# Column norms with a quarter of the array per chunk: 32 columns of ones as weights, 512 moving squares, partial sums added at the end

## The chip, the core and the metric

The kernel runs on one core of a Trainium2 chip. The metric is the device time of one execution in microseconds (us). Five engines work beside each other, each with its own in-order queue: TensorE (PE in the profile; its weight loads are listed apart as PEld), VectorE (DVE), ScalarE (ACT), GpSimd (POOL) and SyncE (SP). Sixteen DMA engines move data between the main memory and the on-chip buffer SBUF. Matmuls write to a second on-chip memory, PSUM, which is read by VectorE and ScalarE.

## The reference

There are four batches. In each, q, k and v have 6400 rows and 256 columns. The columns of q and k are divided by their norms over the 6400 rows, a 256x256 matrix of cosines is formed and turned into weights by a softmax, and v is multiplied by it. A mixture of eight adapters with two experts per row follows.

```python
qn = q / (np.linalg.norm(q, axis=1, keepdims=True) + 1e-06)
kn = k / (np.linalg.norm(k, axis=1, keepdims=True) + 1e-06)
s = kn.transpose(0, 2, 1) @ qn / tau
...                                   # softmax over the last axis: a
x = (v @ a).reshape(B * S, D)
logits = x @ w_gate                   # top 2 of 8, weights w by softmax
out = x + sum over the two experts of w * ((x @ A[e]) @ B[e])
```

The norms are the part of this that the change is about: for each of 256 columns of q and 256 of k, the sum of 6400 squares, in each batch.

## The kernel before

**Tiling.** The 6400 rows of a batch are 50 chunks of 128 rows; the rows lie on the 128 partitions. q and k come in tiles of 10 chunks (`qk`, four buffers), v in tiles of up to 18 chunks (`vt`, three buffers). GpSimd issues these loads, which convert from fp32 to bf16 on the way. Outputs are collected in groups of up to ten chunks (`ys`, nine buffers) and stored by ScalarE's queue, the last ones by SyncE's.

**First part of a batch.** Squares are made for two chunks at a time (`square`, L199), by ScalarE or, in batch 0, in turn by VectorE and ScalarE, into a pool of four tiles `sq` of 128 x (q and k) x 2 chunks x 256. `gram` (L211) adds k-transposed times q of one chunk to the PSUM tile `acc` with two matmuls of 256 moving columns (L217). `norm` (L222) adds the sums of squares of one chunk to the PSUM tile `nrm`. It has two forms. In batch 0 the weights are 128x128 ones and the 512 squares of the chunk (256 of q, 256 of k) move (L228): every partition of `nrm` then holds all 512 sums. In batches 1 to 3 the squares are the weights, four blocks of 128 columns, and one column of ones moves (L234): four matmuls, and the 512 sums lie in four columns of `nrm`, one column of the matrix per partition.

**The chain.** When a batch has all its chunks, seven functions `chain0` to `chain6` turn `acc` and `nrm` into the attention weights and the adapters' weights. `chain0` (L241) takes the logarithm of the sums on ScalarE (L252) and half its exponential (L254), that is the root. In batch 0 VectorE first takes the diagonal of `nrm` (L247) and sums it (L250), to bring the sums to one per partition. `chain1` makes the reciprocals and scales `acc`, `chain2` spreads the norms of q over the partitions with an fp32 matmul of ones (L276), `chain3` takes the exponential, `chain4` to `chain6` transpose and multiply.

**Second part of a batch.** Pairs of chunks of v are transposed on TensorE (L366), copied out of PSUM by VectorE (L377) or ScalarE (L375), multiplied for the gates (L387), for the adapters' z (L472) and for y (L488); z is gated on VectorE (L476), transposed back (L496), and added to y (L508), which ScalarE copies to `ys` (L512).

**Order.** The order of the work is written out by hand: batch 0's first part runs alone, then a loop over "slots" deals out, in each slot, one pair of chunks of the second part of a batch and two or three chunks of the first part of the next. The first parts of batches 1, 2 and 3 lie in the slots 0 to 20, 24 to 45 and 49 to 67 of 100; the functions of the chain follow in the slots behind each. In a slot the squares are put in first, then `chain0` to `chain3`, then the z matmuls, half the slot's `gram` and `norm` work (`gram_part`, L547), the y matmuls and transposes, and the other half. Since each engine's queue is in order, an instruction that waits holds up all that stands behind it there. Stores are held back by seven groups (`DEFER`, L52 and L601) up to the end of batch 3's first part and then let go by and by.

Of the kernel before, what the change touches and what calls it, by code (L numbers as in the profile page):

```python
# [8 lines left out]
FP32 = mybir.dt.float32  # L9
BF16 = mybir.dt.bfloat16  # L10
AX = mybir.AxisListType
OP = mybir.AluOpType
# [4 lines left out]
def kernel(  # L17
# [16 lines left out]
    nc = tc.nc  # L34
    B, N, C = q.shape
    P = 128
    NC = N // P
    CC = C // P
# [23 lines left out]
    const = ctx.enter_context(tc.tile_pool(name="const", bufs=1))  # L62
    qk_pool = ctx.enter_context(tc.tile_pool(name="qkp", bufs=QKB))
    v_pool = ctx.enter_context(tc.tile_pool(name="vp", bufs=VB))
    sq_pool = ctx.enter_context(tc.tile_pool(name="sqp", bufs=4))
# [18 lines left out]
    for b, (first, last) in GRAM.items():  # L84
        n = last - first + 1
# [43 lines left out]
    def load_more(limit=1000):  # L129

        while limit and at_load[0] < len(loads):
            _, kind, b, s, o, parts = loads[at_load[0]]
            if (kind, b, s) not in where:
                n = len(left[kind])
                if n >= bufs[kind] and left[kind][n - bufs[kind]]:
                    return
                where[kind, b, s] = n
                left[kind].append(PC if kind == "qk" else VP[s])
                if kind == "qk":
                    t = qk_pool.tile([P, 2, PC, C], BF16, tag="qk", name="qk")  # L140
                else:
                    t = v_pool.tile([P, max(VP), C], BF16, tag="v", name="vt")
                tiles[kind][b, s] = t
            t = tiles[kind][b, s]
            c0 = s * PC if kind == "qk" else sum(VP[:s])
            for m in parts:
                if kind == "qk":
                    nc.gpsimd.dma_start(t[:, 0, o:o + m, :], q_v[b, :, c0 + o:c0 + o + m, :])  # L148
                    nc.gpsimd.dma_start(t[:, 1, o:o + m, :], k_v[b, :, c0 + o:c0 + o + m, :])
                else:  # L150
                    nc.gpsimd.dma_start(t[:, o:o + m, :], v_v[b, :, c0 + o:c0 + o + m, :])  # L151
                o += m
            at_load[0] += 1
            limit -= 1
# [14 lines left out]
    ones_bf = const.tile([P, P], BF16)  # L169
    nc.vector.memset(ones_bf, 1.0)  # L170
    ones_f = const.tile([P, P], FP32)
    nc.vector.memset(ones_f, 1.0)
    neg_inv_tau = const.tile([P, 1], FP32)
    nc.vector.memset(neg_inv_tau, -inv_tau)
    for c in range(0, FIRST, 2):
# [6 lines left out]
    ident_f = const.tile([P, P], FP32)  # L182
# [14 lines left out]
    acc, nrm, sqs = {}, {}, {}  # L197

    def square(b, c, eng):  # L199

        s, o = divmod(c, PC)
        t = tiles["qk"][b, s]
        sq = sq_pool.tile([P, 2, 2, C], BF16, tag="sq", name="sq")
        sqs[b, c] = sq
        src = t[:, :, o:o + 2, :]
        if eng == "act":
            nc.scalar.activation(sq, src, ACT.Square)  # L207
        else:
            nc.vector.tensor_tensor(out=sq, in0=src, in1=src, op=OP.mult)  # L209

    def gram(b, c):  # L211
        if c == 0:
            acc[b] = ps_acc.tile([P, CC, C], FP32, tag="acc", name="acc")
        s, o = divmod(c, PC)
        t = tiles["qk"][b, s]
        for ic in range(CC):
            nc.tensor.matmul(  # L217
                acc[b][:, ic, :], t[:, 1, o, ic * P:(ic + 1) * P], t[:, 0, o, :],
                start=(c == 0 and ic == 0), stop=(c == NC - 1), skip_group_check=True)
        used("qk", b, c, 1)  # L220

    def norm(b, c):  # L222
        if c == 0:
            nrm[b] = ps_nrm.tile([P, 512], FP32, tag="nrm", name="nrm")
        sq = sqs[b, c - c % 2]
        if b == 0:

            nc.tensor.matmul(nrm[b].rearrange("p (w d) -> p w d", w=2), ones_bf, sq[:, :, c % 2, :],  # L228
                             start=(c == 0), stop=(c == NC - 1))
            return  # L230
        for w in range(2):
            for ic in range(CC):
                j = w * CC + ic
                nc.tensor.matmul(  # L234
                    nrm[b][:, j:j + 1], sq[:, w, c % 2, ic * P:(ic + 1) * P], ones_bf[:, 0:1],
                    start=(c == 0 and j == 0), stop=(c == NC - 1), skip_group_check=True)


    st = {}

    def chain0(b):  # L241
        d = st.setdefault(b, {})
        sums = nrm[b][:, 0:4]
        if b == 0:
            dq = sq_pool.tile([P, 4 * C], BF16, tag="sq", name="dq").bitcast(FP32).rearrange(
                "p (j d) -> p j d", j=4)
            nc.vector.tensor_tensor(out=dq, in0=nrm[b].rearrange("p (j d) -> p j d", j=4),  # L247
                                    in1=ident_f[:, None, :].to_broadcast([P, 4, P]), op=OP.mult)
            sums = const.tile([P, 4], FP32, name="sums")
            nc.vector.tensor_reduce(out=sums, in_=dq, axis=AX.X, op=OP.add)  # L250
        lnn = bat.tile([P, 4], FP32, name="lnn")
        nc.scalar.activation(lnn, sums, ACT.Ln)  # L252
        rt = bat.tile([P, 4], FP32, name="rt")
        nc.scalar.activation(rt, lnn, ACT.Exp, scale=0.5)  # L254
        d["rt"] = rt
# [71 lines left out]
    def chain6(b):  # L327
        d = st[b]
        a_bf = bat.tile([P, CC, C], BF16, name="a_bf")
        for ic in range(CC):  # L330
# [3 lines left out]


    CHAIN = [(chain0, 0.0), (chain1, 0.9), (chain2, 0.75), (chain3, 0.0), (chain4, 0.55),
             (chain5, 0.65), (chain6, 0.5)]


    groups = []  # L340
    for b in range(B):
        f = 0
        for n in [5, 5, 5, 5, 3, 2] if b == B - 1 else [GRP] * (NPAIR // GRP):
            g = {"b": b, "f": b * NPAIR + f, "n": n, "ready": False}
# [187 lines left out]
    for c in range(0, NC, 2):  # L532
        square(0, c, "act" if (c // 2) % 2 else "dve")
        gram(0, c)
        gram(0, c + 1)
        load_more()
        if c >= 4:
            norm(0, c - 4)
            norm(0, c - 3)
    for c in range(NC - 4, NC):  # L540
        norm(0, c)
    for f, _ in CHAIN:
        f(0)
        if f is chain3:
# [2 lines left out]
    def gram_part(items):  # L547
        for b, c in items:
            gram(b, c)
            if c >= 2:  # L550
                norm(b, c - 2)
            if c == NC - 1:
                norm(b, c - 1)
                norm(b, c)

    micro = []
    at_chain = {}
# [14 lines left out]
    zq, dq = None, None  # L572
    while nz < NPT or zq is not None or dq is not None:
# [10 lines left out]
        if f in (chain0, chain1, chain2, chain3):  # L584
            f(fb)
# [5 lines left out]
        if zq is not None:  # L591
            gz_t(zq, "act" if slot >= NPT else "dve")
        gram_part(items[:h])
        if dq is not None:
            y_mm(dq)
# [4 lines left out]
        dq, zq = zq, u  # L600
# [4 lines left out]
        if 0 < slot <= NPT and slot - 1 == groups[slot - 1]["f"] + groups[slot - 1]["n"] - 1:  # L605
# [3 lines left out]
            ops[0][1]()  # L609
            micro += ops[1:]  # L610
        gram_part(items[h:])
        if f in (chain4, chain5, chain6):
            f(fb)
# [42 lines left out]
```

## Time and profile before

| what | value |
|---|---|
| median of 3 runs | 255.92 us (255.84 to 256.08) |
| the profiled execution | 255.87 us |
| its span, first to last instruction | 254.1 us |
| busy: TensorE, VectorE, ScalarE, GpSimd | 220.4, 152.7, 176.1, 33.0 us |
| norm matmuls, batches 1 to 3 (L234) | 600, 35.9 us listed as busy |
| norm matmuls, batch 0 (L228) | 50, 15.8 us listed as busy |
| main memory read and written | 78.91 and 26.21 MB |

The span is what the profile covers; the time has some 1.8 us around it. In the profile the row of digits cuts the span into 40 slices, and each digit is the busy share in tenths. The chain of work goes back from the last instruction to what released each step. A busy time is the sum of listed durations, with overlaps inside a group counted once; the duration of a matmul includes the time until its result is out, so matmuls that follow one another overlap, and what one costs the queue is the distance between the starts.

### The profile page before, as it was taken

The numbers are of one execution on the slowest core, as the hardware profiler recorded it, in microseconds if no ns is written. First come the engines' busy times: TensorE is split into PE (matmuls) and PEld (weight loads), VectorE is DVE, ScalarE is ACT, GpSimd is POOL, SyncE is SP. The second block draws the span as 40 slices with busy tenths as digits, with TensorE's granted clock in tenths as the row PEclk, the third lists the DMA queues.
The fourth block names the chain that finished last, engine by engine and source line by source line (L and its number), as shares of the span: only waits on it lengthen the run. The fifth ranks groups of instructions, "written<-read, shape, count | busy, mean of one in ns | idle before, by whom it ended". The sixth has DMA issues, their size and how long they took to land.

```text
span 254.1 us, 7393 instructions
## 1 busy us (share of the span) xinstructions
PE 220.4 (87%) x3106; PEld 190.2 (75%) x3106; DVE 152.7 (60%) x577; ACT 176.1 (69%) x290; POOL 33.0 (13%) x67
## 2 busy tenths in 40 slices
PE   0787793985999999999999989999999899999950
PEld 0444461775899978989999778989997799998940
DVE  1322235453567678685776876767587876778720
ACT  3434344776488698887878778888867777887860
POOL 8131221112112100110110202000000200000000
PEclk9999998696899999999999999999999999999997
DMA  7999999999999999999999999999999999999995
GB/s 213 223 217 215 212 216 214 213 216 216 210 214 215 223 207 215 218 212 214 215 220 211 214 270 259 236 296 281 255 291 292 389 326 362 414 420 426 423 412 220
DMA packets 13745, 66.80 MB, mean 263 GB/s; under 512 B 2576, under 2 KB 2704, under 8 KB 10384
## 3 DMA queue, kind: packets, MB, share of 16 engines
q0 software_dynamic: 8496, 38.80, 74.8%
q10 hardware_dynamic: 2592, 23.59, 22.4%
q1 hardware_dynamic: 2624, 3.94, 4.7%
q8 instruction: 24, 0.39, 0.6%
q14 instruction: 9, 0.07, 0.1%
HBM read 78.91 MB, written 26.21 MB: 414 GB/s over the span
## 4 chain that ended last, share of the span: by engine, by line
PE 58%; DMA 25%; DVE 7%; ACT 3%; issue 2%; POOL 1%; DVEq 0%; POOLq 0%; ACTq 0%
DMA qk<-in_k_dram 20%; PE y_ps L488 15%; PE acc L217 11%; PE zg L472 7%; PE y_ps L508 7%; PE vT_ps L366 6%; DMA out_dram<-ys 5%; PE zg L496 4%; PE nrm L234 3%; PE vT_ps L387 3%; ACT sq L207 2%; DVE gz L476 2%; ACT ys L512 1%; DVE lm L422 1%; DVE e L418 1%
## 5 line engine op out<-in xcount | busy, mean ns | idle before, releaser
L207 ACT ACTIVATE sq<-qk 128x1024 bf16<-128x1024 bf16 x87 | 89.6, 1054 | 22.1 <-DMA qk<-in_k_dram 16.8
L217 PE MATMUL acc<-qk 128*128 128x256 bf16 x400 | 74.7, 287 | 15.3 <-DMA qk<-in_k_dram 8.8
L512 ACT COPY ys<-y_ps 128x512 f32<-128x512 f32 x100 | 58.8, 588 | 22.9 <-PE y_ps L508 19.7
L488 PE MATMUL y_ps<-a_bf,vT 128*128 128x256 bf16 x400 | 60.3, 273 | 0.3 <-ACT ys L512 0.3
L217 PEld LDWEIGHTS <-qk 128*128 128x128 bf16 x400 | 34.4, 102 | 25.4 <-DMA qk<-in_k_dram 11.8
L476 DVE TENSOR_TENSOR gz<-zg,gate 128x256 bf16<-128x256 f32 x100 | 41.7, 418 | 14.7 <-PE zg L472 13.4
L377 DVE COPY vT<-vT_ps 128x512 bf16<-128x512 bf16 x63 | 26.7, 424 | 28.2 <-PE vT_ps L366 27.6
L234 PEld LDWEIGHTS <-sq 128*128 128x128 bf16 x600 | 36.3, 98 | 7.2 <-ACT sq L207 3.1
L366 PE MATMUL vT_ps<-ident,vt 128*128 128x128 bf16 x400 | 39.5, 223 | 0.9 <-DMA vt<-in_v_dram 0.7
L472 PE MATMUL zg<-wa_sb,vT 128*128 128x128 bf16 x400 | 38.7, 220 | 1.2 <-DVE gzT L502 1.0
L508 PE MATMUL y_ps<-ball_sb,gzT 128*128 128x256 bf16 x200 | 38.2, 273 | 0.0
L234 PE MATMUL nrm<-ones_bf,sq 128*128 128x1 bf16 x600 | 35.9, 165 | 1.2 <-ACT sq L207 1.2
L488 PEld LDWEIGHTS <-vT 128*128 128x128 bf16 x400 | 33.6, 97 | 3.2 <-issue 0.4
L366 PEld LDWEIGHTS <-vt 128*128 128x128 bf16 x400 | 30.2, 99 | 3.4 <-DMA vt<-in_v_dram 0.8
L496 PE MATMUL zg<-ident,gz 128*128 128x128 bf16 x200 | 27.9, 222 | 1.1 <-DVE gz L476 0.6
L375 ACT COPY vT<-vT_ps 128x512 bf16<-128x512 bf16 x37 | 21.7, 587 | 10.3 <-PE vT_ps L366 8.9
L472 PEld LDWEIGHTS <-vT 128*128 128x128 bf16 x400 | 26.1, 97 | 3.4 <-issue 2.2
L502 DVE COPY gzT<-zg 128x256 bf16<-128x256 bf16 x90 | 25.3, 281 | 0.0
L148 POOL DMA_DIRECT2D qk<-in_q_dram x21 | 11.4, 545 | 91.1 <-ACT sq L207 23.6
L209 DVE TENSOR_TENSOR sq<-qk 128x1024 bf16<-128x1024 bf16 x13 | 9.0, 693 | 22.3 <-DMA qk<-in_k_dram 15.4
L496 PEld LDWEIGHTS <-gz 128*128 128x128 bf16 x200 | 15.3, 99 | 2.9 <-DVE gz L476 2.5
L151 POOL DMA_DIRECT2D vt<-in_v_dram x17 | 9.0, 534 | 64.4 <-PE y_ps L508 45.5
(61 smaller groups left out, 183.6 us busy)
## 6 DMA issues: line engine op xcount, KB each, us to landing
out_dram<-ys ACTq DMA_DIRECT2D x18, 1280.0 KB, 13.1
qk<-in_q_dram POOLq DMA_DIRECT2D x18, 640.0 KB, 20.9
qk<-in_k_dram POOLq DMA_DIRECT2D x18, 640.0 KB, 23.1
vt<-in_v_dram POOLq DMA_DIRECT2D x5, 1024.0 KB, 26.9
vt<-in_v_dram POOLq DMA_DIRECT2D x3, 1152.0 KB, 25.3
vt<-in_v_dram POOLq DMA_DIRECT2D x6, 512.0 KB, 22.1
out_dram<-ys SPq DMA_DIRECT2D x3, 512.0 KB, 8.7
out_dram<-ys SPq DMA_DIRECT2D x4, 256.0 KB, 7.6
```

Of the source, the lines that this page charges most:

```text
L207: nc.scalar.activation(sq, src, ACT.Square)
L217: nc.tensor.matmul(acc[b][:, ic, :], t[:, 1, o, ic * P:(ic + 1) * P], t[:, 0, o, :], start=(c == 0 and ic == 0), stop=(c == NC - 1), skip_ ...
L234: nc.tensor.matmul(nrm[b][:, j:j + 1], sq[:, w, c % 2, ic * P:(ic + 1) * P], ones_bf[:, 0:1], start=(c == 0 and j == 0), stop=(c == NC - 1 ...
L366: nc.tensor.matmul(pt[:, ic, sc * P:(sc + 1) * P], vt[:, o + sc, ic * P:(ic + 1) * P], ident, is_transpose=True, start=(i == 0), stop=(i = ...
L377: nc.vector.tensor_copy(dst, src)
L472: nc.tensor.matmul(z[:, sc, :], r["vT"][:, ic, sc, :], st[b]["wa"][:, ic, E:E + ER], start=(sc == 0 and ic == 0), stop=(sc == 1 and ic == ...
L476: nc.vector.tensor_tensor(out=gz.rearrange("p c (e r) -> p c e r", e=E), in0=z.rearrange("p c (e r) -> p c e r", e=E), in1=gr["gate"][:, r ...
L488: nc.tensor.matmul(y[:, sc, :], r["vT"][:, ic, sc, :], st[b]["a"][:, ic, :], start=(sc == 0 and ic == 0), stop=False, skip_group_check=True)
L496: nc.tensor.matmul(gt[:, sc, :], r["gz"][:, sc, :], ident, is_transpose=True, start=(sc == 0), stop=(sc == 1))
L502: nc.vector.tensor_copy(gzT, gt)
L508: nc.tensor.matmul(r["y"][:, sc, :], r["gzT"][:, sc, :], ball_sb, start=False, stop=(sc == 1), skip_group_check=True)
L512: nc.scalar.copy(gr["ys"][:, r["w"]:r["w"] + 2, :], r["y"])
```

## The change

Both forms of `norm` give way to one function, `norms`, for up to four chunks at a time. For each chunk there is one matmul with 32 columns of ones as weights and the chunk's 512 squares moving. The four chunks of a call use the four quarters of the array's columns (`tile_position=(0, g)`, g = 0, 32, 64, 96), and write to the four quarters of `nrm`'s partitions. Over a batch, each partition of a quarter adds up all 512 sums of a quarter of the chunks. The call is made once in four chunks, for chunks that lie two to five back, and once for the last two of the batch.

`chain0` then copies `nrm` to SBUF (tile `part`, from the pool of the squares), and four fp32 matmuls with the moving column `share_f`, which holds 1/32, add the 128 partitions of each block of 128 sums: each quarter is there 32 times over. The sums are written to the first four columns of `nrm`, one per partition, as ScalarE's logarithm needs them. VectorE's diagonal and sum of batch 0 are gone.

```diff
+    share_f = const.tile([P, 1], FP32)
+    nc.vector.memset(share_f, 1.0 / 32)
...
-    def norm(b, c):
-        if c == 0:
+    def norms(b, c0, n):
+        if c0 == 0:
             nrm[b] = ps_nrm.tile([P, 512], FP32, tag="nrm", name="nrm")
-        sq = sqs[b, c - c % 2]
-        if b == 0:
-            nc.tensor.matmul(nrm[b].rearrange("p (w d) -> p w d", w=2), ones_bf, sq[:, :, c % 2, :],
-                             start=(c == 0), stop=(c == NC - 1))
-            return
-        for w in range(2):
-            for ic in range(CC):
-                j = w * CC + ic
-                nc.tensor.matmul(
-                    nrm[b][:, j:j + 1], sq[:, w, c % 2, ic * P:(ic + 1) * P], ones_bf[:, 0:1],
-                    start=(c == 0 and j == 0), stop=(c == NC - 1), skip_group_check=True)
+        for c in range(c0, c0 + n):
+            g = 32 * (c - c0)
+            nc.tensor.matmul(nrm[b][g:g + 32, :].rearrange("p (w d) -> p w d", w=2),
+                             ones_bf[:, 0:32], sqs[b, c - c % 2][:, :, c % 2, :], start=(c < 4),
+                             stop=(c >= NC - 4), skip_group_check=True, tile_position=(0, g))
...
     def chain0(b):
         d = st.setdefault(b, {})
+        part = sq_pool.tile([P, 4 * C], BF16, tag="sq", name="part").bitcast(FP32).rearrange(
+            "p (j d) -> p j d", j=4)
+        nc.scalar.copy(part, nrm[b].rearrange("p (j d) -> p j d", j=4))
         sums = nrm[b][:, 0:4]
-        if b == 0:
-            dq = sq_pool.tile([P, 4 * C], BF16, tag="sq", name="dq").bitcast(FP32).rearrange(
-                "p (j d) -> p j d", j=4)
-            nc.vector.tensor_tensor(out=dq, in0=nrm[b].rearrange("p (j d) -> p j d", j=4),
-                                    in1=ident_f[:, None, :].to_broadcast([P, 4, P]), op=OP.mult)
-            sums = const.tile([P, 4], FP32, name="sums")
-            nc.vector.tensor_reduce(out=sums, in_=dq, axis=AX.X, op=OP.add)
+        for j in range(4):
+            nc.tensor.matmul(sums[:, j:j + 1], part[:, j, :], share_f, start=(j == 0), stop=(j == 3),
+                             skip_group_check=True)
         lnn = bat.tile([P, 4], FP32, name="lnn")
         nc.scalar.activation(lnn, sums, ACT.Ln)
...
         load_more()
-        if c >= 4:
-            norm(0, c - 4)
-            norm(0, c - 3)
-    for c in range(NC - 4, NC):
-        norm(0, c)
+        if c % 4 == 0 and c:
+            norms(0, c - 4, 4)
+    norms(0, NC - 2, 2)
...
             gram(b, c)
-            if c >= 2:
-                norm(b, c - 2)
+            if c % 4 == 1 and c > 1:
+                norms(b, c - 5, 4)
             if c == NC - 1:
-                norm(b, c - 1)
-                norm(b, c)
+                norms(b, c - 1, 2)
```

## The prediction

> **What bounds the kernel now.** I read the page's slices first, then the windows of 6 us with their DMA share, the chain of work, and the order of TensorE's work around the norm matmuls. The slices show two resources that are full at once: the sixteen DMA engines from start to end, and TensorE from about 60 us on.
>
> ```profile
> span 254.1 us, 7393 instructions
> ...
> PE   0787793985999999999999989999999899999950
> ...
> DMA  7999999999999999999999999999999999999995
> ...
> PE 58%; DMA 25%; DVE 7%; ACT 3%; issue 2%; POOL 1%; DVEq 0%; POOLq 0%; ACTq 0%
> ```
>
> The windows near the end (columns: stretch, its length, busy time of PE, PEld, DVE, ACT and POOL, granted clock, DMA share, GB/s) show which of the two ends the run.
>
> ```profile
> 192.00:198.00 6.00, 5.47 (x85) 4.71 (x83) 4.39 (x19) 4.10 (x12) 0.00 (x0) 1.00 1.02 305
> 198.00:204.00 6.00, 5.33 (x82) 4.41 (x80) 5.15 (x25) 4.51 (x10) 1.58 (x3) 1.00 1.01 388
> ...
> 240.00:246.00 6.00, 5.13 (x53) 4.05 (x51) 2.58 (x13) 4.89 (x12) 0.00 (x0) 1.00 1.00 413
> 246.00:252.00 6.00, 0.00 (x0) 0.00 (x0) 0.00 (x0) 0.09 (x1) 0.00 (x0) 0.86 0.83 334
> ```
>
> TensorE is done at 245.5 us and the DMA engines drain stores until about 252.7 us: the DMA share is at or above 1.00 in every window from 6 to 246 us and falls to 0.83 only at the very end. So the bytes set a floor: work taken from TensorE can win little, because the same loads and stores must still pass. Work put on TensorE is free only as long as its end stays ahead of the DMA backlog. The last output stores show that lead:
>
> ```profile
> L516 SPq DMA_DIRECT2D out_dram<-ys x7: 332/354/867, 238.0 to 246.1; - x7
> ...
> DMA to landing us min/median/max: 6.9/8.3/9.3
> ```
>
> A 512 KB load at the start, with empty queues, landed in 3.6 us (the stage load of q). Half of that at 413 GB/s is 0.6 us, so a 256 KB store without a backlog takes about 3.0 us (an estimate from those two rows). The last stores take at least 6.9, so TensorE can end some 3.9 us later before the end moves. Before that, the chain of work holds one wait on a store, at which ScalarE's copy waited for a y buffer:
>
> ```profile
> 181.41 13.06 DMA out_dram<-ys
> ...
> 194.55 0.59 ACT ys L512
> ```
>
> **The norm matmuls, batches 1 to 3.** What is removed is 600 matmuls with one moving column (L234), listed at 165 ns each; but those are pipelined, and the order in time gives their real price:
>
> ```profile
> 103.95 0.38 PE L217 MATMUL acc<-qk 128*128 128x256 bf16 x2
> 104.17 0.24 PE L234 MATMUL nrm<-ones_bf,sq 128*128 128x1 bf16 x4
> 104.28 0.60 PE L488 MATMUL y_ps<-a_bf,vT 128*128 128x256 bf16 x4
> ...
> 37.15 1.46 PE L228 MATMUL nrm<-sq,ones_bf 128*128 128x512 bf16 x6
> ```
>
> The four matmuls of one chunk start at 104.17 and the next work starts at 104.28, so a chunk costs 0.105 us (other quartets of that stretch give 0.10 to 0.11), four chunks 0.42 us, and the 150 chunks 15.8 us: far less than the 35.9 us of busy time in the group's row. In their place come, per batch, 12 groups of four matmuls with 512 moving columns and 32 weight columns, and one group of two: 36 and 3 in all. No row shows a matmul on a quarter of the array. The nearest is L228 with the same 512 columns on the whole array: six in 1.46 us, the last with its listed 0.379, so (1.46 - 0.38) / 5 = 0.216 us apart.
>
> Low end of a group: the four streams run at once and cost one, 0.216 us, which is -0.20 per group and -7.3 us for 36; it cannot be less, as one stream of 512 columns must pass. High end: they follow one another, 0.864, and the array empties on the way in and on the way out. The price of emptying I take from the gram row: two start 0.1075 us apart (104.17 - 103.95 = 0.22 for two), and the pair is listed with 0.38, so about 0.165 us lies between the last column in and the end. Twice that makes 1.19 us, +0.77 per group, +28 us. I take one stream and both emptyings, 0.216 + 0.33 = 0.546 us: the stream by its nearest row, and an emptying on either side because, as I assume, the weight loads of whole-array matmuls, which are now loaded ahead (PEld is busy beside PE in every window), meet a different division of the array at both borders of each group. That is +0.126 x 36 = +4.5 us, and for the three pairs (0.546 - 0.21) x 3 = +1.0 us. Sum +5.5 us.
>
> Trainium skill, "TensorEngine Tiling (Array Packing)", Key Properties: tiles of one mode work independently, but changing the mode drains TensorE. That rule speaks against this change, which changes mode 78 times in these three batches; the page gives no time for a drain and no run here shows one yet. "TensorE: Matmul & The Clock Gate", Part 3, has tiles starting about 4 ns apart: 0.216 + 0.012 = 0.23 us for a group, which without any drain would be (0.23 - 0.42) x 36 = -6.8 us in place of my +4.5.
>
> **The end of the norms, chain0.** New on this path: a ScalarE copy of 128x512 from PSUM, then four fp32 matmuls with one column, which stand in TensorE's in-order queue ahead of the slot's z, y and transpose matmuls. So TensorE waits for ScalarE, where now it goes straight on:
>
> ```profile
> 87.59 0.44 PE L234 MATMUL nrm<-ones_bf,sq 128*128 128x1 bf16 x12
> 87.89 0.38 PE L472 MATMUL zg<-wa_sb,vT 128*128 128x128 bf16 x4
> ...
> 88.07 0.17 ACT L252 ACTIVATE lnn<-nrm 128x4 f32<-128x4 f32 x1 [0.41 <-PE nrm L234]
> ...
> L276 PEld LDWEIGHTS nrm<-dg,ones_f x8: 186/189/192, 41.6 to 190.7; 128*128 128x128 f32 x8
> ```
>
> ScalarE was idle 0.41 us before its Ln, so the copy starts when the norms end. TensorE's wait: 0.165 until the last norm is out, 0.04 to ScalarE, 0.588 for the copy (the L512 row, same shape), 0.05 back: 0.85 us. The fp32 matmuls: four calls of L276 are eight rows, so a call is two passes and there are eight here; two L276 weight loads are listed with 0.30 us together and 0.189 singly, 0.11 us apart, so 0.9 us. Ends: 0.2 us (eight at the 25 ns of L234: twelve in 0.30 us) and 1.5 us (eight at 0.189, nothing overlapped). Sum 1.75 us, between 1.05 and 2.35, for each of three batches: +5.25 us. Behind it wait, on ScalarE, Ln and Exp, the vT copy and the ys copy; on VectorE the chain1 work (L260 began 1.4 us after its input, so it still has cover). All of them wait for TensorE anyway, and all shift together, so I count the stall once.
>
> **Batch 0.** 50 matmuls of 0.216 us (0.43 at the half rate of the early chunks) become 13 groups; VectorE's L247 and L250 (0.69 us each) give way to the copy and the fp32 matmuls. All of this is hidden: TensorE is next let go by a load, the chain shows 23.65 us of waiting for in_k until 59.77 us. Should that cover go, the stage is still no worse than about 1 us.
>
> **Moves that cost nothing.** Each group waits for two squares that are older than before, or as old; squared tiles are held up to two chunks longer in a pool of four, so that ScalarE may wait for TensorE where it now waits 2.3 us in all; ScalarE is busy 4 to 5.3 us of 6, which covers it. The loads' issue on POOL follows TensorE's release of buffers, but from 12 to 155 us they land 16 to 29 us after issue, so delays of a few us leave the queues full. The extra memset, 59 ns, lies beside the first loads.
>
> **The sum.** TensorE: +5.5 + 5.25 = +10.8 us up to 190 us. Of the windows' TensorE idle time between 66 and 246 us (about 3.9 us, 1.2 of it around the wait at 194) I let half be used up: -1.9. The lead at the end takes 3.9. Left: +5.0 us. The profiled execution took 255.87 us (span 254.1 and 1.8 around it), the median is 255.92, so no correction: 255.9 + 5.0 = 260.9 us.
>
> **Rivals.** (a) Hidden: the group costs between 0.28 and 0.43 us, so that TensorE's change is between 0 and +5.8 us and the DMA backlog covers it. For it: the DMA share above 1.00 everywhere. Against: it needs emptyings well under the 0.165 us of the row. 255.5 to 256.4 us. (b) The other side, faster: groups under 0.28 us pay for the chain0 stalls (36 x 0.14 = 5.0), TensorE ends earlier, and the last stores queue more tightly. The only thing to win is the slack of the drain: 0.17 of 6 us in the last window, 1.0 us: 254.9 us. (c) The quarters do not overlap: 0.864 us a group with little emptying is +16 us, with both +28; with the pairs (about +1) and chain0, less the 5.8 covered: 272 to 284 us. For it: each group's matmuls each have their own weight load between them; against: nothing in the trace.
>
> **How the numbers follow.** What can be told from no change here is about 0.2%, 0.5 us. My case, delays of 6 to 20 us on TensorE, 257 to 270 us: 0.52. (a) 0.18, same. (b) 0.14, faster. (c) 0.16. Slower is my case and (c): 0.68. The range runs from 255.0 to 271: it leaves out the best of (b) and (c), about 0.2. My case alone: 257 to 268.
>
> **What would show it.** In the order of TensorE's work after: the distance from a group's first quarter matmul to the next full one (0.55 us by my count; 0.25 in (b), 0.9 or more in (c)); the gap ahead of the L246 matmuls, 0.85 us, and their length, 0.9; TensorE's end near 254 instead of 245.5; last stores that land in 3 to 4 us; DMA shares under 1.00 after 200 us. I am wrong if TensorE's delay is taken up elsewhere, or if the quarters start within nanoseconds of each other with no gap at their borders.

## The result: 259.67 us, and the profile after

The changed kernel takes 259.67 us (259.57 to 260.74) against 255.97 us: the ratio is 1.0153 with a 95% interval of 1.0130 to 1.0176. It is slower, by 3.7 us; the forecast was 260.9 us. The page of the profile after, the same lines as before:

```profile
span 257.8 us, 6564 instructions
...
PE   0769394896999899999999989999989999999970
...
DMA  7999999999999999999999999999999899999994
...
PE 57%; DMA 19%; DVE 8%; ACT 8%; issue 3%; POOL 2%; ACTq 0%; DVEq 0%; POOLq 0%
```

There is one new digit that matters: the DMA row has an 8 in the slice at about 200 us. The windows show it (columns as above: stretch, length, PE, PEld, DVE, ACT, POOL, clock, DMA share, GB/s).

```profile
186.00:192.00 6.00, 5.88 (x83) 4.47 (x80) 4.84 (x20) 4.46 (x8) 0.53 (x1) 1.00 0.96 301
192.00:198.00 6.00, 5.38 (x74) 5.05 (x75) 2.92 (x12) 4.14 (x10) 0.00 (x0) 1.00 0.91 228
198.00:204.00 6.00, 5.85 (x80) 4.93 (x78) 5.20 (x24) 5.13 (x14) 0.28 (x1) 1.00 0.87 354
204.00:210.00 6.00, 5.38 (x82) 4.71 (x82) 5.05 (x24) 4.44 (x10) 1.31 (x3) 1.00 0.96 297
...
246.00:252.00 6.00, 3.87 (x39) 2.89 (x36) 1.63 (x7) 3.90 (x9) 0.00 (x0) 1.00 1.00 407
```

Before, these four stretches had shares of 1.00, 1.02, 1.01 and 1.03; the first and the last of them, from the kernel before:

```profile
186.00:192.00 6.00, 6.00 (x88) 5.43 (x87) 4.86 (x21) 5.15 (x12) 0.50 (x1) 1.00 1.00 296
204.00:210.00 6.00, 5.89 (x92) 5.43 (x90) 4.40 (x20) 4.43 (x10) 0.00 (x0) 1.00 1.03 331
```

Now they have 0.96, 0.91, 0.87 and 0.96. The difference is 0.36 of 6 us, 2.2 us of DMA time lost in the middle of the run. That is not the whole 3.7 us: summed over all windows of 6 us, the transfers took 260.5 us of DMA time before and 261.9 now, and why they took longer is open. A finer view of 186 to 210 us (40 slices, tenths of DMA time) shows holes; the first line is the kernel before, in a fence of its own:

```profile
DMA  8969999899999889999999999999999999999999
```

```profile
DMA  9999977699989999927999939999935999999499
```

**The quarter groups** do what they say. TensorE's work in order of time, kernel after:

```profile
105.68 0.38 PE L219 MATMUL acc<-qk 128*128 128x256 bf16 x2
105.99 0.40 PE L231 MATMUL nrm<-sq,ones_bf 128*32 128x512 bf16 x4
106.32 0.40 PE L469 MATMUL zg<-wa_sb,vT 128*128 128x128 bf16 x4
```

Four matmuls of 512 columns together take 0.40 us, where each single one of such a group is listed with 0.39: they run at once. The gram pair in front takes 0.215 us in the queue, to 105.895. So the group costs 106.32 - 105.895 = 0.425 us: 0.095 ahead of it, 0.216 for a stream, and 0.11 behind. The old price for four chunks was 0.42. The weight loads in the same stretch stand idle just before the group and just after it, so at both borders they no longer run ahead of the matmuls:

```profile
105.99 0.10 PEld L231 LDWEIGHTS <-ones_bf 128*32 128x32 bf16 x4 [0.21 <-issue]
106.32 0.23 PEld L469 LDWEIGHTS <-vT 128*128 128x128 bf16 x4 [0.23 <-issue]
```

**The stall of chain0** is where the time goes. TensorE, and in the second fence ScalarE, at the end of batch 1's norms:

```profile
86.40 0.38 PE L219 MATMUL acc<-qk 128*128 128x256 bf16 x2
86.71 0.61 PE L231 MATMUL nrm<-sq,ones_bf 128*32 128x512 bf16 x6
88.05 1.05 PE L246 MATMUL nrm<-share_f,part 128*128 128x1 f32 x8 [0.73 <-ACT part L242]
88.97 0.38 PE L469 MATMUL zg<-wa_sb,vT 128*128 128x128 bf16 x4
```

```profile
87.42 0.59 ACT L242 COPY part<-nrm 128x512 f32<-128x512 f32 x1 [0.73 <-PE nrm L231]
```

The gram pair is through at 86.62; z starts at 88.97, 2.35 us later, where before it was 0.30 us (twelve old matmuls from 87.59, z at 87.89). The net stall is 2.05 us, and it is 2.04 and 2.05 in batches 2 and 3. The 2.35 us are 0.52 for the last group of four and the pair behind it (one border of 0.095 and two streams of 0.216), 0.91 for the wait until the copy is there, and 0.92 for the eight fp32 passes. The clock was full in this stretch.

**From the stalls to the end.** The starts of the same instructions in the two profiles, before and after:

| mark | before | after | later by |
|---|---|---|---|
| last gram pair of batch 1 | 87.37 | 86.40 | -0.97 |
| z after chain0, batch 1 | 87.89 | 88.97 | +1.08 |
| last gram pair of batch 2 | 139.39 | 140.55 | +1.16 |
| z after chain0, batch 2 | 139.91 | 143.11 | +3.20 |
| last gram pair of batch 3 | 187.58 | 190.96 | +3.38 |
| z after chain0, batch 3 | 188.10 | 193.53 | +5.43 |
| last loads of v issued | 198.97 | 203.72 | +4.75 |
| last copy to ys | 245.51 | 250.24 | +4.73 |
| span | 254.1 | 257.8 | +3.7 |

The lead of 0.97 us at the start goes with the clock: at 60 to 66 us the granted clock was 0.50 in the profiled execution before (first fence) and 1.00 in the one after.

```profile
60.00:66.00 6.00, 6.00 (x61) 5.07 (x60) 2.10 (x6) 3.72 (x4) 1.48 (x3) 0.50 1.06 217
```

```profile
60.00:66.00 6.00, 5.37 (x78) 4.05 (x79) 2.85 (x9) 4.75 (x6) 1.29 (x3) 1.00 1.05 214
```

It is not a gain of the change: in run 7 below, with the same norms and a clock of 0.52 in that stretch, batch 1's last norms start at 88.20 us, 1.5 us later than the 86.71 of the changed kernel. Between the stalls, with eleven groups each time, the delay grows by 0.08 and 0.18 us; the stalls move it by two microseconds each. And the three last loads of v wait for TensorE (GpSimd's view, kernel after):

```profile
189.55 0.53 POOL L151 DMA_DIRECT2D vt<-in_v_dram  x1 [16.93 <-PE y_ps L505]
203.72 1.59 POOL L151 DMA_DIRECT2D vt<-in_v_dram  x3 [13.64 <-PE y_ps L505]
```

The delay of TensorE thus becomes a delay of loads, and as stores are held back at that time, the DMA engines run dry. What is issued between 186 and 200 us lands sooner than before, which is what an emptier queue would give. The median times from issue to landing of what is issued in that stretch (count, size, us), first in the kernel before, then after:

```profile
out_dram<-ys ACTq DMA_DIRECT2D x4, 1280.0 KB, 11.8
vt<-in_v_dram POOLq DMA_DIRECT2D x1, 1024.0 KB, 15.5
```

```profile
out_dram<-ys ACTq DMA_DIRECT2D x2, 1280.0 KB, 5.6
vt<-in_v_dram POOLq DMA_DIRECT2D x1, 1024.0 KB, 7.9
```

### The profile page after: what moved, and what is told of

The parts are those of the page before. It is cut to its first block, busy times and chain, and to the rows that moved or that the text cites. A ratio compares the mean times of both kernels' runs of the same rounds, so it can differ in the third digit from the quotient of the medians.

```text
span 257.8 us, 6564 instructions
## 1 busy us (share of the span) xinstructions
PE 222.2 (86%) x2688; PEld 175.8 (68%) x2688; DVE 151.1 (59%) x576; ACT 178.8 (69%) x294; POOL 32.6 (13%) x67
## 4 chain that ended last, share of the span: by engine, by line
PE 57%; DMA 19%; DVE 8%; ACT 8%; issue 3%; POOL 2%; ACTq 0%; DVEq 0%; POOLq 0%
PE y_ps L485 14%; PE acc L219 10%; DMA qk<-in_k_dram 10%; DMA vt<-in_v_dram 9%; PE zg L469 7%; PE y_ps L505 6%; PE vT_ps L363 6%; PE nrm L231 4%; PE zg L493 4%; PE vT_ps L384 3%; ACT sq L209 2%; DVE gz L473 2%; ACT ys L509 2%; ACT vT L372 2%; PE nrm L246 1%
## 5 line engine op out<-in xcount | busy, mean ns | idle before, releaser
L219 PEld LDWEIGHTS <-qk 128*128 128x128 bf16 x400 | 36.7, 106 | 28.4 <-DMA qk<-in_k_dram 12.0
L485 PEld LDWEIGHTS <-vT 128*128 128x128 bf16 x400 | 36.0, 98 | 6.2 <-issue 3.0
L363 PEld LDWEIGHTS <-vt 128*128 128x128 bf16 x400 | 30.9, 99 | 4.6 <-DMA vt<-in_v_dram 1.2
L469 PEld LDWEIGHTS <-vT 128*128 128x128 bf16 x400 | 29.2, 98 | 6.9 <-issue 5.0
L231 PE MATMUL nrm<-sq,ones_bf 128*32 128x512 bf16 x200 | 21.9, 420 | 0.6 <-ACT sq L209 0.6
L505 PEld LDWEIGHTS <-gzT 128*128 128x128 bf16 x200 | 16.0, 98 | 0.4
```

Of the source, the lines that this page charges most:

```text
L219: nc.tensor.matmul(acc[b][:, ic, :], t[:, 1, o, ic * P:(ic + 1) * P], t[:, 0, o, :], start=(c == 0 and ic == 0), stop=(c == NC - 1), skip_ ...
L231: nc.tensor.matmul(nrm[b][g:g + 32, :].rearrange("p (w d) -> p w d", w=2), ones_bf[:, 0:32], sqs[b, c - c % 2][:, :, c % 2, :], start=(c < 4),
L363: nc.tensor.matmul(pt[:, ic, sc * P:(sc + 1) * P], vt[:, o + sc, ic * P:(ic + 1) * P], ident, is_transpose=True, start=(i == 0), stop=(i = ...
L469: nc.tensor.matmul(z[:, sc, :], r["vT"][:, ic, sc, :], st[b]["wa"][:, ic, E:E + ER], start=(sc == 0 and ic == 0), stop=(sc == 1 and ic == ...
L485: nc.tensor.matmul(y[:, sc, :], r["vT"][:, ic, sc, :], st[b]["a"][:, ic, :], start=(sc == 0 and ic == 0), stop=False, skip_group_check=True)
L505: nc.tensor.matmul(r["y"][:, sc, :], r["gzT"][:, sc, :], ball_sb, start=False, stop=(sc == 1), skip_group_check=True)
```

## The experiments

Two theories stood at first. A: the stalls in chain0 cost it all. B: the borders of the quarter groups, and squares held longer, cost it. The first four runs tell them apart; each ratio is to the kernel before on the same chip. Code that is cut in the edits is marked `...`.

**1. The end of the norms left out.**

```diff
-        part = sq_pool.tile(...)
-        nc.scalar.copy(part, nrm[b]...)
         sums = nrm[b][:, 0:4]
-        for j in range(4):
-            nc.tensor.matmul(sums[:, j:j + 1], part[:, j, :], share_f, ...)
```

> The changed kernel without the end of the norms: no copy of the partial sums, no fp32 matmuls; the logarithm reads the first four columns of the partial sums, so the norms are not the reference's (that addition is left out). The quarter matmuls stay. Theory A (the end of the norms costs it all, three stalls of TensorE of about 2.05 us; the quarter groups cost what the old norm matmuls did): 255.7 to 256.4 us. Theory B (the borders of the quarter groups, and squares that are held longer, cost it): 259 us or more.

Measured 256.26 us, ratio 1.0005 (0.9993 to 1.0018); one of the ten executions took 703.42 us, for a reason that the record does not show. With all quarter groups in place nothing is lost: B falls.

**2. The stall alone, on the kernel before.**

```diff
         sums = nrm[b][:, 0:4]
+        if b > 0:
+            part = sq_pool.tile(...)
+            nc.scalar.copy(part, acc[b]...)
+            for j in range(4):
+                nc.tensor.matmul(nrm[b][:, 4 + j:5 + j], part[:, j, :], share_f, ...)
```

> The kernel before, with its own norm matmuls, and in batches 1 to 3 the ScalarE copy (of acc, 128x512) and four fp32 matmuls with one column put into chain0, whose result nothing uses. Theory A: 258.8 to 259.9 us, with a TensorE gap of about 2 us at each of the three places. Theory B: 256.0 to 256.8 us.

Measured 259.68 us, ratio 1.0154 (1.0114 to 1.0194), the whole loss. The agreement to the last tenth is partly chance. Here a stall is only 1.5 us net in batch 1 (the old matmuls start at 86.35 and take 0.30, z starts at 88.15), as the copy of `acc` need not wait for the norms; but after batch 2's stall TensorE's clock fell for some microseconds:

```profile
138.00:142.00 4.00, 3.55 (x60) 3.32 (x58) 2.02 (x8) 2.10 (x5) 1.58 (x3) 0.91 1.03 211
142.00:146.00 4.00, 4.00 (x32) 3.33 (x31) 2.57 (x14) 2.67 (x7) 0.00 (x0) 0.67 1.05 214
```

The granted clock is 0.67 from 142 to 146 us, against 1.00 in the kernel after. The last loads of v came at 203.61 us, as late as in the kernel after.

**3. chain0 cut in two, the matmuls one slot later.**

```diff
         nc.scalar.copy(part, nrm[b]...)
+        d["part"] = part
+
+    def chain0b(b):
+        d = st[b]
+        part = d["part"]
         sums = nrm[b][:, 0:4]
...
-    CHAIN = [(chain0, 0.0), (chain1, 0.9), ...
+    CHAIN = [(chain0, 0.0), (chain0b, 0.0), (chain1, 0.9), ...
...
```

> The changed kernel with chain0 cut in two: the copy in its slot, the fp32 matmuls, logarithm and root one slot later, all that follows one slot later too. TensorE no longer waits for the copy, but still does the fp32 matmuls (0.92 us a batch). Theory A: of three times 2.05 us some 3 us are left, 256.2 to 257.8 us. Theory B: 259 to 260 us.

Measured 256.08 us, ratio 0.9995 (0.9985 to 1.0004). The computation and the fp32 matmuls are the same as in the changed kernel, and the loss is gone; less is left than the 0.2 to 1.8 us I had expected.

```profile
87.37 0.61 PE L231 MATMUL nrm<-sq,ones_bf 128*32 128x512 bf16 x6
89.14 0.95 PE L251 MATMUL nrm<-share_f,part 128*128 128x1 f32 x8
89.95 0.38 PE L474 MATMUL zg<-wa_sb,vT 128*128 128x128 bf16 x4
```

No wait stands at the fp32 matmuls now (no bracket). They still take 0.81 us of TensorE's queue per batch, from 89.14 to 89.95; it is hidden.

**4. The same, in bf16.**

```diff
-    share_f = const.tile([P, 1], FP32)
+    share_f = const.tile([P, 1], BF16)
...
-        part = sq_pool.tile(...).bitcast(FP32)...
+        part = sq_pool.tile(...)[:, 0:2 * C]...
...
```

> As the run before, with the partial sums copied to bf16 and 1/32 in bf16, so that the four matmuls are one pass each (some 0.1 us a batch, by the 25 ns of the old one-column matmuls). Theory A: 255.6 to 256.4 us, no different from the kernel before, since the groups are neutral and the DMA floor is the same. Theory B: 258.8 to 260 us.

Measured 256.23 us, ratio 1.0014 (1.0000 to 1.0028): with the cheapest ending nothing is gained over run 3. TensorE's time is not what is short here.

**Why is a stall not covered by the end?** My prediction let the backlog of stores at the end cover 3.9 us of any delay (theory E). Against it now stood theory S: what covers a delay is the smallest backlog on the way behind it, which I took to be near zero at 186 to 210 us.

**5 and 6. The same work on TensorE, early and late.** The y matmuls of eight pairs are done twice, in the kernel before:

```diff
             y_mm(dq)
+            if 30 <= dq < 38:        # late: 84 <= dq < 92
+                again(dq)            # the same four matmuls, started afresh
```

> The kernel before, with the four y matmuls of eight pairs in the middle of batch 1 (pairs 30 to 37) done twice: 8 x 0.43 = 3.5 us more on TensorE long before 186 us. Theory S (what counts is the smallest DMA backlog on the way, which is near zero at 186 to 210 us): 1 to 3 us longer, 257 to 259 us, with DMA shares under 1.00 at 186 to 210 us. Theory E (the lead of 3.9 us at the end takes it, wherever the delay arises): 255.8 to 256.5 us.

> The same 3.5 us of doubled y matmuls, but for pairs 84 to 91, after 220 us. Theory S and theory E alike: the backlog of stores at the end covers it, 255.8 to 256.6 us. If work late costs as much as early (257 us or more), both are wrong about the lead.

Early: 257.89 us, ratio 1.0066 (1.0041 to 1.0090). Late: 256.11 us, ratio 1.0000 (0.9991 to 1.0009). The same 3.5 us cost 1.8 us or nothing, by their place alone. DMA time in the early run, 186 to 210 us in 40 slices, and its last loads:

```profile
DMA  9999996997999999996999999999989999399999
```

```profile
201.97 1.59 POOL L151 DMA_DIRECT2D vt<-in_v_dram  x3 [11.92 <-PE y_ps L515]
```

The holes are there again, with no quarter group and no chain0 stall in the kernel. In the late run the last loads are issued at 199.27 us, and the last copies end three and a half microseconds later than before (249.56 against 246.09), yet the end does not move: there the backlog does cover, and the shortest landing of the last stores falls from 6.9 to 3.7 us. E falls for early work and holds for late work; what S forecast came true for both. That the place of a delay decides is shown. That the backlog before is near zero at 186 to 210 us is not: stores issued at 186 to 200 us landed after 11.8 us there, and after 5.6 in the changed kernel, whose engines ran dry. By these rows some 6 us lay ahead of them (an estimate, the difference of the two), and why so little of it was free is open.

**7. Stores held back less.**

```diff
-    DEFER = 7
+    DEFER = 5
```

> The changed kernel, stores held back by five groups instead of seven, so that two more groups have gone out before the hole. Theory S says the hole at 186 to 210 us is a lack of issued transfers while loads wait for TensorE; stores that went out earlier only move bytes ahead, and loads are then behind them: between 257.5 us (hole filled) and 260 us (nothing won). Theory E: no change, 259.7 us.

Measured 260.71 us, ratio 1.0179 (1.0162 to 1.0196): nothing won, and beyond the upper end I gave. The profiled execution, at 259.48 us the fastest of five, has smaller holes in the middle (shares of 1.02, 1.03, 1.01 and 0.98), but its last loads come later still:

```profile
206.84 1.59 POOL L151 DMA_DIRECT2D vt<-in_v_dram  x3 [13.64 <-PE y_ps L505]
```

They are 3.1 us later than in the changed kernel. Of this, 1.5 us are there from batch 1's last norms on and go with the lower clock at 60 to 66 us. The other 1.6 come between batches 2 and 3, where TensorE waits for a load of v, a wait that the changed kernel does not have; and the hole is now at the end:

```profile
176.16 0.40 PE L363 MATMUL vT_ps<-ident,vt 128*128 128x128 bf16 x4 [2.41 <-DMA vt<-in_v_dram]
```

```profile
240.00:246.00 6.00, 6.00 (x91) 5.61 (x89) 4.36 (x21) 4.96 (x13) 0.00 (x0) 1.00 0.64 267
```

The DMA share is 0.64 there, and the last stores land after as little as 2.7 us: no backlog is left to cover the end. Stores that go earlier fill one hole and open another. This run does not tell S from E.

**8. A shorter stall.** Run 4's bf16 edit without the cut:

```diff
-    share_f = const.tile([P, 1], FP32)
+    share_f = const.tile([P, 1], BF16)
...
```

> The changed kernel with bf16 partial sums and bf16 1/32, chain0 not cut: the stall keeps its wait for the copy and loses most of the 0.92 us of fp32 passes, so each of the three stalls is about 1.25 us instead of 2.05, 2.4 us less in all. With one us of delay on TensorE costing 0.7 to 0.8 us as in the changed kernel: 257.5 to 258.3 us.

Measured 257.57 us, ratio 1.0054 (1.0039 to 1.0069). TensorE at batch 1:

```profile
87.17 0.38 PE L219 MATMUL acc<-qk 128*128 128x256 bf16 x2
87.47 0.61 PE L231 MATMUL nrm<-sq,ones_bf 128*32 128x512 bf16 x6
88.82 0.25 PE L246 MATMUL nrm<-share_f,part 128*128 128x1 bf16 x4 [0.74 <-ACT part L242]
88.94 0.38 PE L469 MATMUL zg<-wa_sb,vT 128*128 128x128 bf16 x4
```

From 87.385 to 88.94 are 1.56 us, 1.26 net of the old 0.30; the passes take 0.12 us in place of 0.92. In the changed kernel the wait for the copy (0.91) and the fp32 passes (0.92) weigh the same; this run leaves the wait, and more than half of the loss is gone.

**9, 10 and 11. Which stall counts?** chain0 is cut for some batches alone; the others keep their stalls.

```diff
+    def chain0all(b):
+        chain0(b)
+        chain0b(b)
...
     for b, (first, last) in GRAM.items():
-        for i, (f, us) in enumerate(CHAIN):
+        steps = CHAIN if b == B - 1 else [(chain0all, 0.0)] + CHAIN[2:]   # 10: b < B - 1; 11: b == 2
+        for i, (f, us) in enumerate(steps):
             at_chain[last + 1 + i] = (f, us, b)
...
```

> The changed kernel with chain0 cut in two, as in the deferred run, for batch 3 alone; batches 1 and 2 keep their stalls of about 2.05 us. Theory S with equal stalls: the last loads of v, issued at 203.7 us in the changed kernel and at 199.0 before, come at about 202.5 us, and the time is 257.8 to 259 us. Rival L (only the last stall counts, as it stands right at the hole of 186 to 210 us): 255.8 to 256.6 us.

> The changed kernel with chain0 cut in two for batches 1 and 2; batch 3 keeps its stall. Theory S (all TensorE delay ahead of the last loads of v counts, beyond about one us): one stall of 2 us is left, the last loads at 200 to 201.5 us, 256.0 to 257.2 us, and the first store's issue is short. If the place of the stall did not matter and each cost a third: 257.2 us.

> The changed kernel with chain0 cut in two for batch 2 alone; batches 1 and 3 keep their stalls. Theory S: two stalls, some 4 us of delay less the one us that is free, the last loads at 201.5 to 203 us, 257 to 258.8 us. Rival Q (the issue of the first store, which took 4.3 us in the changed kernel and 0.4 before, and which stands behind batch 2's chain0, is what costs): with the stall ahead of it gone the issue is short, and the time 255.8 to 256.6 us.

| stalls left in batches | us | ratio (interval) | last loads at | span |
|---|---|---|---|---|
| none (run 3) | 256.08 | 0.9995 (0.9985 to 1.0004) | 199.28 | 254.4 |
| 3 | 256.14 | 1.0008 (0.9998 to 1.0018) | 199.89 | 254.3 |
| 1 and 3 | 257.76 | 1.0065 (1.0047 to 1.0083) | 202.42 | 256.4 |
| 1 and 2 | 260.12 | 1.0159 (1.0139 to 1.0180) | 203.56 | 258.4 |
| 1, 2 and 3 (the change) | 259.67 | 1.0153 (1.0130 to 1.0176) | 203.72 | 257.8 |

The last two columns are from the profiled execution, which took 256.14, 256.04, 258.21, 260.19 and 259.57 us in the order of the rows. Batch 3's stall by itself costs nothing (its last loads, at 199.89, came just ahead of the 200 to 201.5 that I expected). Beside it, batch 1's stall costs 1.6 us, and batch 2's another 1.9: rival L, that only the last one counts, falls. The run with batch 3 cut missed what I expected of S (257.8 to 259). Two things in its profile bear on it. Its TensorE came to batch 1's last norms 0.67 us later than in the changed kernel (87.38 against 86.71; the granted clock at 60 to 66 us was 0.72 against 1.00), so its loads were hardly earlier. And the cut of batch 3 has a price of its own, a wait of TensorE at the changeover: it is busy 4.47 of 6 us at 204 to 210 in this run, and 4.19 at 198 to 204 in run 3, against 5.63 and 5.34 in runs 11 and 10, where batch 3 is not cut. The last 0.6 us of its span are argued from this, not shown.

Rival Q, that the long issue of the first store is to blame, falls with the run that cuts batch 2 alone. Its first store, on ScalarE's queue, and that of the changed kernel:

```profile
149.63 0.38 ACTq L531 DMA_DIRECT2D out_dram<-ys  x1
```

```profile
148.63 4.34 ACTq L526 DMA_DIRECT2D out_dram<-ys  x1
```

The issue is short there, and the time is still 1.7 us up.

**12. Groups of eight chunks.** To see whether less work on TensorE would be worth something, on run 4's kernel:

```diff
-    sq_pool = ctx.enter_context(tc.tile_pool(name="sqp", bufs=4))
+    sq_pool = ctx.enter_context(tc.tile_pool(name="sqp", bufs=6))
...
-            g = 32 * (c - c0)
+            g = 32 * ((c - c0) % 4)
...
-            if c % 4 == 1 and c > 1:
-                norms(b, c - 5, 4)
+            if c % 8 == 1 and c > 1:
+                norms(b, c - 9, 8)
...
```

> The deferred kernel with bf16 partial sums, and groups of eight chunks, two per quarter, so that the border is paid half as often: a group of eight at about 0.1 + 0.33 + 0.22 = 0.65 us against 0.84 us for eight chunks before, some 3.4 us less on TensorE over batches 1 to 3. (Six tiles for the squares; s_sb is written over tk and a_bf over ae to make room.) If the bytes set the floor: 255.5 to 256.4 us, no different from the kernel before. If TensorE's time is what counts: 252.5 to 254 us.

Measured 256.37 us, ratio 1.0021 (1.0006 to 1.0036).

```profile
100.31 0.38 PE L219 MATMUL acc<-qk 128*128 128x256 bf16 x2
100.62 0.61 PE L231 MATMUL nrm<-sq,ones_bf 128*32 128x512 bf16 x8
101.17 0.18 PE L317 MATMUL wa_ps<-wg_sb,aT 128*128 128x8 bf16 x1
```

Eight chunks cost 101.17 - 100.525 = 0.645 us against 0.84, as worked out, so 3.5 us are saved on TensorE over eighteen such groups; the kernel is no faster. No run beat the kernel before.

## Why the prediction was right, and which of its terms were not

The time, 259.67 us, lies 1.2 us from the forecast and in the range, and the main line of the argument held: the stalls in chain0 are what costs, work on TensorE does not come back as time saved, and delay on TensorE is charged beyond a free part. That the number came so close is partly luck. TensorE's delay was put 4.4 us too high (10.8, measured 6.4), and what covers it 3.1 us too high (5.8, measured 2.7). With the delay as measured and the cover as assumed the sum would have been 256.5 us, beside rival (a) and under the 257 us at which I let my own case begin.

- **The groups.** I took 0.546 us, one stream and two emptyings of 0.165 us, +4.5 us in all. Measured: 0.425 us, so the two borders cost 0.095 and 0.11 us, and 36 groups cost some +0.2 us. The streams do run at once, as rivals (a) and (b) had it; 0.425 is in the bounds of (a), over the 0.28 of (b), and (c) is out. Nor are there 78 changes of mode: the pair follows the last group of four directly, which makes 72. Trainium skill, "TensorEngine Tiling (Array Packing)", Key Properties, has TensorE drain at each change of mode; the trace shows a gap at each, of a tenth of a microsecond, and does not tell a drain from a weight load (0.093 us listed) that no longer runs ahead. "TensorE: Matmul & The Clock Gate", Part 3, has tiles that start some 4 ns apart; four listed with 0.40 us together and 0.39 each put it at about 3 ns here.
- **chain0.** 1.75 us a batch; measured 0.91 for the wait (0.85 predicted) and 0.92 for the passes from 88.05 to 88.97 (0.9 predicted), 1.83. The stall of 2.05 holds also the last six chunks' matmuls, 0.52, less the 0.30 of the twelve old ones; by my prices for a group and a pair the same stretch would have been 2.54 us.
- **TensorE in all.** +10.8 us predicted; measured 3 x 2.05 and 0.3 between the stalls, +6.4. From this come off 0.97 us that go with the clock at 60 to 66 us, on which nothing had been said, and 0.7 us behind the last stall: +4.73 at the last copy. I had let 1.9 us be taken up on the way.
- **The lead at the end.** This is the step that failed: "The lead at the end takes 3.9". Measured: the end moved by 3.7 us where TensorE's moved by 4.73, so the lead took 1.0. The shortest landing of the last stores shows the same, 6.9 before and 5.9 after, where I had forecast 3 to 4:

```profile
DMA to landing us min/median/max: 5.9/7.3/8.6
```

The lead at the end is made after 200 us, when the stores held back are let go. A delay that comes before this delays loads, stores and lead together, and in the changed kernel the DMA engines ran dry at 186 to 210 us. I had the rows of 192 to 204 us in front of me, with shares of 1.02 and 1.01, and read them as full; the share alone could not tell, as it is 1.00 to 1.02 at 222 to 246 us too, where late work costs nothing. My rows on landing times, 16 to 29 us, stopped at 155 us, ahead of the stretch that mattered. Runs 5 and 6 show the difference: 1.8 us or nothing for the same 3.5 us of work.

So the forecast of +5.0 us was the difference of +10.8 and 5.8 of cover, and the measured +3.7 us that of 6.4 and 2.7, of which 0.97 goes with the clock of the two profiled executions and not with the change. Over the runs the date of the last loads of v orders the spans: up to 199.9 us (before, runs 1, 3, 4, 6, 12 and the one that keeps batch 3's stall) 254.1 to 254.5; 201.8 to 202.4 (runs 8, 5, and stalls in 1 and 3) 255.8 to 256.4; 203.6 to 203.7 (run 2, the change, stalls in 1 and 2) 257.7 to 258.4. In this order the first microsecond is free, and each one beyond it costs about 0.8 to 1.2. Run 7 does not fit, 206.84 us with a span of 257.7; its DMA time is lost at the end.

## What to carry to other kernels

A reduction that costs the same in its loop can lose everything at its end. An in-order engine that must wait for another engine's copy pays the wait and the arithmetic behind it: cheaper arithmetic won back more than half of the loss here (run 8), and the dependent work moved one step back in the queue won back all of it, with its arithmetic kept (run 3). Where one resource is full from start to end, a backlog at the end does not cover a delay that comes long before it: try the same work early and late, and look at the time from issue to landing beside the share. Price short matmuls by the distance between their starts: 600 of them that were listed with 35.9 us of busy time cost 15.8.

## What the runs showed that I had not expected

- The issue of the first store on ScalarE's queue took 4.34 us in the changed kernel, and 4.05, 4.02 and 4.41 in runs 2, 8 and 9; it took 0.34 to 0.38 in all others. It is long in the runs in which batch 2's chain0 stalls, except run 7, whose first store goes out ahead of that stall. Why is open. It cost TensorE little: from batch 2's last norms to batch 3's are 48.19 us before, and 50.42 after, of which 2.05 are the stall.
- A stall of TensorE can be followed by a lower clock: 0.67 from 142 to 146 us in run 2. In the changed kernel, with a longer stall, it was 1.00 in that stretch, so this depends on more than the length of the stall.
- A one-column matmul on fp32 weights of 128x128 costs 0.23 us in the queue (0.92 us for four calls of two passes behind a wait, 0.81 in run 3 without one), a one-column one on bf16 weights 0.026 (0.105 for four).
